# Q's fourth weight block on GpSimd's queue, and ahead of the third in the projection

## The chip, the core and the metric

The kernel runs on one core of a Trainium2 chip. The core has five engines that run side by side and meet through semaphores: TensorE (PE; its weight loads are listed as PEld), VectorE (DVE), ScalarE (ACT), GpSimd (POOL) and SyncE (SP). An engine takes its instructions in the order in which the program gives them, and so does the queue from which an engine issues its transfers. The metric is the device time of one execution in microseconds. All times within an execution count from the start of its span, the time from its first instruction to its last.

## What is computed

Two blocks read the same layer-normalised input, and their sum is added to the input. Block A is linear attention with 32 heads of 16 columns; block B is a gated feed-forward network. All inputs are bf16; S = 2048 rows, D = 512, F = 1792.

```python
xn = _layernorm(x, axis=-1)
return x + _A_ref(xn, A_wqkv, A_wo) + _B_ref(xn, B_w_gate, B_w_up, B_w_down)

# _A_ref: q, k, v = split(x @ wqkv)
phi = lambda t: jnp.where(t > 0, t + 1, jnp.exp(t)) + 1e-6
pq, pk = phi(q), phi(k)
kv = jnp.einsum("bhsd,bhse->bhde", pk, v)
z = jnp.einsum("bhsd->bhd", pk)
num = jnp.einsum("bhqd,bhde->bhqe", pq, kv)
den = jnp.einsum("bhqd,bhd->bhq", pq, z)[..., None] + 1e-6
o = num / den            # then o @ wo

# _B_ref
g = _silu(x @ w_gate)
u = x @ w_up
return (g * u) @ w_down
```

The change lies in q = xn @ wqkv[:, 0:512], for the first two tiles of rows.

## The kernel before

The 2048 rows are worked in 16 tiles of 128. The program is written out by hand: a helper (`K.op`, `K.dma`) appends each instruction to its engine's list in the order of the calls and puts a wait in front of it wherever an operand was written, or a buffer is still read, by another engine. Nothing reorders the lists afterwards; `emit` (L90) writes them out, and each wait is a `wait_ge` on one semaphore. Every DMA has a semaphore of its own.

The first stage loads x and the weights and makes K's and Q's projections. The weight matrix of K, and that of Q, is loaded in blocks of 128 of its 512 rows, since a projection sums over four such blocks: `wqkv_load(eng, h, name, i, c0, n, after)` (L211) loads the n blocks from c0 on, and `xload` (L205) loads tiles of x. Each block of a weight and each lone tile of x is 128 KB. `after` is a list of results that the issue waits for. SP's queue issues, in order: x 0; wk 0 and 1 in one transfer; wk 2; x 2; wq 0; wq 1; x 3; wq 2; wq 3; x 4; x 5; x 6 and 7 in one. ACT's queue issues x 1 and wk 3. GpSimd's queue issues no transfer; its work up to there is four small set-up instructions (L236 to L244), and next on it stand `eps(0)` (L315), `rstd_of(0)` (L325) and `nbias(0)` (L398), which make the scale of tile 0 from the statistics that VectorE takes with `bns` (L299) and `agg` (L302).

The first four tiles take a faster way in than the rest. Their x is centred or corrected but not yet scaled, transposed (into `xcT`), and multiplied with the weights; the scale `rstd` comes in later, when ScalarE reads the product (`first_ek`, `first_pk`, `first_pq`, L579 to L601). `proj_part(t, wname, c, pos)` (L520) is one matmul of 128x512: block c of the weight for tile t. `pos` is its place in the sum over four: 0 clears the PSUM bank, 3 closes it. K's product of tile t lies in bank 2·(t mod 2), Q's in the bank after it. Tile 2 and the ones after it use `proj_first` (L506) and `proj` (L493), which run over the blocks by themselves.

TensorE's order around the change is: K of tile 0 and K of tile 1 (blocks 0, 1, 3, 2), Q's blocks 0 and 1 for tile 1 and then for tile 0, four transposes of tile 2 (`tp_first`, L464), Q's blocks 2 and 3 for both tiles (these four are L731 to L735), then K and Q of tile 2 (L511), and the first accumulation of xn and phi(K) (`gtacc`, L645, matmuls at L649). ScalarE reads Q of tile 0 with `first_pq(0)`, which stands between the last two of the four matmuls in the program.

From tile 4 on a loop projects K and Q of a tile, takes their exponentials, and accumulates. The feed-forward stage (L844 on) and the output (L1038 on) follow. Neither is touched.

Of the kernel before, what the change touches and what calls it, by code (L numbers as in the profile page):

```python
# [109 lines left out]
def bass_parallel_sum__linear_attn_block__swiglu_ffn__prompt_kernel(  # L110
# [13 lines left out]
    pe, act, dve, pool, sp = nc.tensor, nc.scalar, nc.vector, nc.gpsimd, nc.sync  # L124
    bf, f32 = dt.bfloat16, dt.float32

    with contextlib.ExitStack() as es:
# [65 lines left out]
        def bk(i):  # L193
            return ("bank", i)
# [5 lines left out]
        def rows(v, t0, n):  # L200
            if t0 < NLONE:
                return v[t0 * P:(t0 + n) * P, :].rearrange("(t p) d -> p t d", p=P)
            return v[NLONE * P:, :].rearrange("(p t) d -> p t d", t=NT - NLONE)[:, t0 - NLONE:t0 - NLONE + n, :]

        def xload(eng, h, t0, n, after=()):  # L205
            K.dma(
                eng, lambda: h.dma_start(x_sb[:, t0:t0 + n, :], rows(xin, t0, n)),
                r=list(after), w=[("x", t0 + i) for i in range(n)],
            )

        def wqkv_load(eng, h, name, i, c0, n, after=()):  # L211
            K.dma(
                eng,
                lambda: h.dma_start(
                    wqkv_sb[:, c0:c0 + n, i * D:(i + 1) * D],
                    A_wqkv[c0 * P:(c0 + n) * P, i * D:(i + 1) * D].rearrange("(c p) f -> p c f", p=P),
                ),
                r=list(after), w=[(name, c) for c in range(c0, c0 + n)],
            )
# [37 lines left out]
        wqkv_load("sp", sp, "wq", 0, 1, 1)  # L257
        xload("sp", sp, 3, 1)
        wqkv_load("sp", sp, "wq", 0, 2, 1)
        wqkv_load("sp", sp, "wq", 0, 3, 1)  # L260
        xload("sp", sp, 4, 1)
        xload("sp", sp, 5, 1)
        xload("sp", sp, 6, 2)

        cw = nc.const_aps.tensor(1.0, (P, P), bf)
        cx = nc.const_aps.tensor(1.0, (P, 512), bf)
# [35 lines left out]
        def agg(t):  # L302
            K.op("dve", lambda: dve.bn_aggr(mv[:, t, :], stats[:, t, :]), r=[("st", t)], w=[("mv", t)])
# [202 lines left out]
        def proj_first(t, wname, h):  # L506
            lo, b = (D, kb(t)) if wname == "wk" else (0, qb(t))
            K.op(
                "pe",
                [  # L510
                    (lambda c=c: pe.matmul(  # L511
                        banks[b], xcT[:, NDC * t + c, :], wqkv_sb[:, c, lo:lo + D],
                        start=(c == 0), stop=(c == NDC - 1),
                    ))
                    for c in (2 * h, 2 * h + 1)
                ],
                r=[("xcT", t, i) for i in (2 * h, 2 * h + 1)] + [(wname, i) for i in (2 * h, 2 * h + 1)], w=[bk(b)],
            )

        def proj_part(t, wname, c, pos):  # L520
            lo, b = (D, kb(t)) if wname == "wk" else (0, qb(t))
            K.op(
                "pe",
                lambda: pe.matmul(  # L524
                    banks[b], xcT[:, NDC * t + c, :], wqkv_sb[:, c, lo:lo + D],
                    start=(pos == 0), stop=(pos == NDC - 1),
                ),
                r=[("xcT", t, c), (wname, c)], w=[bk(b)],
            )

        def kb(t):
            return 2 * (t % 2)

        def qb(t):
            return 2 * (t % 2) + 1
# [61 lines left out]
        def first_pq(t):  # L597
            K.op(
                "act", lambda: act.activation(pkq[:, t, 1, :], banks[qb(t)], ACT.Identity, scale=rstd[:, t:t + 1]),
                r=[bk(qb(t)), ("rstd", t)], w=[("pq", t)],  # L600
            )  # L601
# [126 lines left out]
        agg(5)  # L728
        bns(6)
        agg(6)  # L730
        proj_part(0, "wq", 2, 2)  # L731
        proj_part(1, "wq", 2, 2)
        proj_part(0, "wq", 3, 3)
        first_pq(0)
        proj_part(1, "wq", 3, 3)  # L735
        proj_first(2, "wk", 0)
        proj_first(2, "wk", 1)
        eps_two(1, "pool")
# [413 lines left out]
```

## Time and profile before

| What | us |
|---|---|
| median of three runs | 210.12 (210.02 to 210.15) |
| the profiled execution's own time | 210.52 |
| its span | 209.3 |
| TensorE busy in it | 205.5 (98%) |
| VectorE / ScalarE / GpSimd busy | 120.1 / 71.0 / 72.1 |

The profile is of one execution. A row of a timeline gives the start, the length, the engine, the line of the program, the operation, what it writes and reads, and how many instructions are merged in the row; in brackets stands how long the engine was idle before it and what ended that. An SPq or ACTq row is the issue of a transfer, and the transfer itself lands later; the list of issues gives the time from the start of the issue to the landing. Matmuls overlap each other in the pipeline, so the length of one (0.38 us for 128x512) is more than the step from one to the next; the ends of matmuls are modelled. Some matmul records can be missing from a trace.

### The profile page before, as it was taken

The numbers are of one execution on the slowest core, as the hardware profiler recorded it, in microseconds if no ns is written. First come the engines' busy times: TensorE is split into PE (matmuls) and PEld (weight loads), VectorE is DVE, ScalarE is ACT, GpSimd is POOL, SyncE is SP. The second block draws the span as 40 slices with busy tenths as digits, with TensorE's granted clock in tenths as the row PEclk, the third lists the DMA queues.
The fourth block names the chain that finished last, engine by engine and source line by source line (L and its number), as shares of the span: only waits on it lengthen the run. The fifth ranks groups of instructions, "written<-read, shape, count | busy, mean of one in ns | idle before, by whom it ended". The sixth has DMA issues, their size and how long they took to land.

```text
span 209.3 us, 2808 instructions
## 1 busy us (share of the span) xinstructions
PE 205.5 (98%) x997; PEld 94.7 (45%) x1016; DVE 120.1 (57%) x246; ACT 71.0 (34%) x125; POOL 72.1 (34%) x91
## 2 busy tenths in 40 slices
PE   8999999999999999999999999999999999999996
PEld 3444444444444444444444444444444444444444
DVE  4899988336365874637355746365556545374122
ACT  4877666966643331312112312213031213121000
POOL 2627977568032543223041422240424132221200
DMA  6764644894796011010201110102011010110101
GB/s 198 228 176 77 128 99 100 253 368 157 204 357 47 12 38 25 28 25 25 52 0 50 28 29 21 50 0 53 6 44 25 27 28 25 49 30 25 50 28 50
DMA packets 30287, 16.84 MB, mean 80 GB/s; under 512 B 20928, under 2 KB 29632, under 8 KB 30272
## 3 DMA queue, kind: packets, MB, share of 16 engines
q1 hardware_dynamic: 29984, 16.39, 30.1%
q10 hardware_dynamic: 288, 0.26, 0.4%
q8 instruction: 8, 0.13, 0.3%
q14 instruction: 7, 0.06, 0.1%
HBM read 9.70 MB, written 2.10 MB: 56 GB/s over the span
## 4 chain that ended last, share of the span: by engine, by line
PE 96%; DVE 2%; issue 1%; POOL 1%; DVEq 0%
PE psum L849 44%; PE psum L1054 23%; PE psum L497 10%; PE psum L1043 7%; PE psum L649 6%; PE psum L524 2%; PE psum L511 2%; PE psum L272 1%; POOL prod L998 1%; PE psum L433 0%; PE psum L421 0%; DVE pkq L573 0%; DVE den L1006 0%; DVE pkq L870 0%; DVE eq L564 0%
## 5 line engine op out<-in xcount | busy, mean ns | idle before, releaser
L864 ACT ACTIVATE sg<-psum 128x512 bf16<-128x512 f32 x56 | 33.4, 598 | 106.0 <-PE psum L849 103.6
L849 PE MATMUL psum<-xnT,wg_sb 128*128 128x512 bf16 x222 | 57.2, 379 | 0.2 <-issue 0.2
L849 PE MATMUL psum<-xnT,wu_sb 128*128 128x512 bf16 x216 | 55.8, 379 | 0.4
L998 POOL TENSOR_TENSOR prod<-pkq,zb 128x512 f32<-128x512 bf16 x16 | 18.6, 1161 | 55.9 <-DVE pkq L573 55.9
L849 PEld LDWEIGHTS psum<-xnT,wu_sb 128*128 128x128 bf16 x224 | 21.9, 98 | 26.4
L849 PEld LDWEIGHTS psum<-xnT,wg_sb 128*128 128x128 bf16 x224 | 21.8, 98 | 26.2 <-issue 0.2
L1067 DVE TENSOR_TENSOR out_sb<-psum,x_sb 128x512 bf16<-128x512 f32 (+2 forms) x17 | 11.2, 660 | 35.9 <-PE psum L1054 35.9
L1022 POOL TENSOR_TENSOR pqn<-pkq,rden 128x512 bf16<-128x512 bf16 x16 | 16.9, 1056 | 36.6 <-DVE rden L1016 36.6
L870 DVE TENSOR_TENSOR pkq<-psum,sg 128x512 bf16<-128x512 f32 x28 | 19.2, 686 | 17.1 <-PE psum L849 14.6
L870 DVE TENSOR_TENSOR xn_sb<-psum,sg 128x512 bf16<-128x512 f32 x28 | 18.8, 671 | 14.2 <-PE psum L849 13.6
L1054 PE MATMUL psum<-wd_sb,xn_sb 128*128 128x512 bf16 (+2 forms) x126 | 25.7, 355 | 0.0
L1054 PE MATMUL psum<-wd_sb,pkq 128*128 128x512 bf16 x108 | 25.1, 379 | 0.2
L497 PE MATMUL psum<-wqkv_sb,xnT 128*128 128x512 bf16 x95 | 22.5, 379 | 0.1
L641 POOL TENSOR_TENSOR zacc<-zacc,pkq 128x512 f32<-128x512 f32 x15 | 17.3, 1156 | 5.0 <-DVE ek L564 4.6
L1054 PEld LDWEIGHTS psum<-wd_sb,xn_sb 128*128 128x128 bf16 x126 | 11.8, 98 | 12.5
L1054 PEld LDWEIGHTS psum<-wd_sb,pkq 128*128 128x128 bf16 x112 | 11.0, 98 | 13.2
L1043 PE MATMUL psum<-m_sb,eq 128*128 128x512 bf16 (+2 forms) x67 | 16.4, 366 | 0.1
L649 PE MATMUL psum<-pkq,xn_sb 128*128 128x512 bf16 x61 | 15.5, 379 | 0.1
L497 PEld LDWEIGHTS psum<-wqkv_sb,xnT 128*128 128x128 bf16 x96 | 9.4, 98 | 11.3
L1006 DVE TENSOR_REDUCE den<-prod 128x32 f32<-128x512 f32 x16 | 10.9, 684 | 5.9 <-POOL prod L998 5.9
L573 DVE SCALAR_TENSOR_TENSOR pkq<-pkq,eq 128x512 bf16<-128x512 bf16 x16 | 11.1, 692 | 0.6
L300 DVE BATCH_NORM_STATS2 stats<-x_sb 128x6 f32<-128x512 bf16 x16 | 10.8, 678 | 0.6 <-DMA x_sb<-in_A_x_dram 0.6
(75 smaller groups left out, 140.0 us busy)
## 6 DMA issues: line engine op xcount, KB each, us to landing
out_dram<-out_sb SPq DMA_DIRECT2D x15, 128.0 KB, 1.7
wg_sb<-in_B_w_gate_dram SPq DMA_DIRECT2D x2, 896.0 KB, 8.1
wu_sb<-in_B_w_up_dram SPq DMA_DIRECT2D x2, 896.0 KB, 6.3
wd_sb<-in_B_w_down_dram SPq DMA_DIRECT2D x1, 1792.0 KB, 11.1
x_sb<-in_A_x_dram SPq DMA_DIRECT2D x5, 256.0 KB, 3.3
x_sb<-in_A_x_dram SPq DMA_DIRECT2D x5, 128.0 KB, 3.2
wqkv_sb<-in_A_wqkv_dram SPq DMA_DIRECT2D x5, 128.0 KB, 3.5
wqkv_sb<-in_A_wqkv_dram SPq DMA_DIRECT2D x1, 512.0 KB, 8.2
```

The source lines that it names most:

```text
L497: (lambda c=c: pe.matmul(banks[b], xnT[:, c, t * P:(t + 1) * P], wqkv_sb[:, c, lo:lo + D], start=(c == 0), stop=(c == NDC - 1),))
L573: lambda: dve.scalar_tensor_tensor(out=dst, in0=src, scalar=0.0, in1=e, op0=ALU.max, op1=ALU.add,),
L641: lambda: pool.tensor_tensor(out=zacc[:, :], in0=zacc[:, :], in1=pk, op=ALU.add),
L649: (lambda c=c: pe.matmul(banks[4 + c], xn_sb[:, t, c * P:(c + 1) * P], pkq[:, t, 0, :], start=(t == 0), stop=(t == NT - 1),))
L849: (lambda c=c: pe.matmul(banks[b], w_sb[:, c, fc * P:(fc + 1) * P], xnT[:, c, C * 512:(C + 1) * 512], start=(c == 0), stop=(c == NDC - 1),))
L864: lambda: act.activation(sg[:, j % NSG, :], banks[gb], ACT.Silu),
L870: lambda: dve.tensor_tensor(out=hT(C, fc), in0=banks[ub], in1=sg[:, j % NSG, :], op=ALU.mult,),
L998: lambda: pool.tensor_tensor(out=p, in0=pkq[:, t, 1, :], in1=zb[:, :], op=ALU.mult),
L1022: lambda: pool.tensor_tensor(out=pqn[:, t % NPN, :].rearrange("p (i g h e) -> p g i h e", i=NB, g=NG, e=DH), in0=pkq[:, t, 1, :].rearrange ...
L1043: (lambda g=g: pe.matmul(dst, pqnT(t)[:, g, :], m_sb[:, g, lo:hi], start=(g == 0), stop=False,))
L1054: (lambda fc=fc: pe.matmul(dst, hT(C, fc)[:, jj * P:(jj + 1) * P], wd_sb[:, fc, lo:hi], start=False, stop=(fc == NFC - 1),))
L1067: lambda: dve.tensor_tensor(out=o, in0=src, in1=x_sb[:, t, lo:hi], op=ALU.add),
```

## The change

The load of Q's fourth block (wq 3) leaves SP's queue, where it stood ahead of x 4, and goes to GpSimd's. There it waits until x 0 has landed. The four matmuls of Q's last two blocks for tiles 0 and 1 change places: block 3 is now the third of the sum, and block 2 the fourth, which closes it.

```diff
         wqkv_load("sp", sp, "wq", 0, 2, 1)
-        wqkv_load("sp", sp, "wq", 0, 3, 1)
         xload("sp", sp, 4, 1)
         xload("sp", sp, 5, 1)
         xload("sp", sp, 6, 2)
+        wqkv_load("pool", pool, "wq", 0, 3, 1, [("x", 0)])
...
-        proj_part(0, "wq", 2, 2)
-        proj_part(1, "wq", 2, 2)
-        proj_part(0, "wq", 3, 3)
+        proj_part(0, "wq", 3, 2)
+        proj_part(1, "wq", 3, 2)
+        proj_part(0, "wq", 2, 3)
         first_pq(0)
-        proj_part(1, "wq", 3, 3)
+        proj_part(1, "wq", 2, 3)
```

The new issue stands behind its four set-up instructions in its list and ahead of `eps(0)`.

## The prediction

> **What bounds the kernel now.** I read the busy times first, then a table of stretches (stretch and its length, then busy us of PE, PEld, DVE, ACT and POOL with instruction counts, granted clock, DMA share, GB/s).
>
> ```profile
> PE 205.5 (98%) x997; PEld 94.7 (45%) x1016; DVE 120.1 (57%) x246; ACT 71.0 (34%) x125; POOL 72.1 (34%) x91
> ```
>
> ```profile
> 4.35:12.00 7.65, 7.60 (x37) 3.55 (x37) 6.75 (x21) 6.28 (x13) 4.62 (x10) 1.00 0.79 228
> 12.00:50.00 38.00, 37.84 (x175) 17.24 (x177) 27.56 (x64) 27.62 (x50) 26.70 (x38) 1.00 0.67 177
> 50.00:100.00 50.00, 49.63 (x271) 22.68 (x275) 30.35 (x55) 15.93 (x28) 15.60 (x15) 1.00 0.34 82
> 100.00:150.00 50.00, 49.74 (x228) 22.64 (x232) 27.58 (x52) 10.16 (x17) 13.04 (x12) 1.00 0.12 30
> 150.00:207.40 57.40, 57.14 (x279) 26.92 (x282) 26.07 (x49) 8.96 (x15) 11.36 (x11) 1.00 0.13 33
> ```
>
> TensorE is busy in all but 1.1 us of the 203 us from 4.35 to 207.40. Busy alone could hide stalls, since matmuls overlap, so I went to the list of waits (engine and line, what it waited for: total, times, longest), asked for PE from 4.5 us to the end. It has one entry:
>
> ```profile
> PE psum L849 <- issue: 0.2, 1, 0.2
> ```
>
> The kernel is therefore bound by TensorE's own rate from its first projection on. An edit that removes no matmul can gain only from a gap ahead of that, or lose by making a new one. Now the place of the edit: the chain of work (start, length, what) and PE's timeline.
>
> ```profile
> 8.24 0.22 PE psum L469 x4
> 8.47 0.86 PE psum L524 x4
> 9.33 1.73 PE psum L511 x8
> ```
>
> ```profile
> 8.25 0.10 PEld L524 LDWEIGHTS psum<-wqkv_sb,xcT 128*128 128x128 bf16 x1
> ...
> 8.57 0.10 PEld L524 LDWEIGHTS psum<-wqkv_sb,xcT 128*128 128x128 bf16 x1 [0.17 <-DMA wqkv_sb<-in_A_wqkv_dram]
> ...
> 8.30 1.03 PE L524 MATMUL psum<-wqkv_sb,xcT 128*128 128x512 bf16 x4
> ```
>
> The four L524 matmuls are wq 2 for tiles 0 and 1, then wq 3 for both: the instructions that the change reorders. They take 0.86 us in the chain, 0.215 each, and the eight after them 1.73, 0.216 each. So the wait for wq 3 that the trace shows (0.17 us at the weight load of 8.57) costs TensorE nothing: that load ends at 8.67, and its matmul is third of the four, due at 8.30 + 2 × 0.216 = 8.73. This is the wait that the change could remove, and it is already hidden, by some 0.06 us.
>
> **The change part by part.** *Removed:* one issue on SP. Its issues stand in these rows (merged where they follow each other; the one of 4.60, wq 3 alone, takes 0.43 us):
>
> ```profile
> 2.23 0.43 SPq L207 DMA_DIRECT2D x_sb<-in_A_x_dram  x1
> 2.70 0.91 SPq L214 DMA_DIRECT2D wqkv_sb<-in_A_wqkv_dram  x2
> 3.65 0.43 SPq L207 DMA_DIRECT2D x_sb<-in_A_x_dram  x1
> 4.12 0.91 SPq L214 DMA_DIRECT2D wqkv_sb<-in_A_wqkv_dram  x2
> ...
> 4.60 0.43 SPq L214 DMA_DIRECT2D wqkv_sb<-in_A_wqkv_dram  x1
> ...
> 5.07 1.39 SPq L207 DMA_DIRECT2D x_sb<-in_A_x_dram  x3
> ```
>
> x 4 to x 7 are issued 5.07 − 4.60 = 0.47 us earlier. VectorE waits for x 4:
>
> ```profile
> 8.90 0.69 DVE L300 BATCH_NORM_STATS2 stats<-x_sb 128x6 f32<-128x512 bf16 x1 [0.59 <-DMA x_sb<-in_A_x_dram]
> ```
>
> Up to 0.47 of that 0.59 may go, but no PE wait hangs on it: worth 0.
>
> *Added on GpSimd:* a wait for x 0 and one issue. x 0 has landed when its first reader starts, 2.95.
>
> ```profile
> 2.95 0.42 DVE L391 SCALAR_TENSOR_TENSOR scr<-x_sb 128x256 bf16<-128x256 bf16 x1 [1.15 <-DMA x_sb<-in_A_x_dram]
> ...
> 1.27 0.29 POOL L244 TENSOR_SCALAR_AFFINE_SELECT ident<-ident 128x128 bf16<-128x128 bf16 x1 [0.20 <-POOL nhalf L240]
> 4.84 0.23 POOL L319 TENSOR_SCALAR vpe<-mv 128x1 f32<-128x1 f32 x1 [3.27 <-DVE mv L303]
> 5.15 0.57 POOL L328 TENSOR_TENSOR rstd<-vpe,nhalf 128x1 f32<-128x1 f32 x1
> ...
> 6.55 0.69 ACT L581 ACTIVATE ek<-psum,rstd 128x512 bf16<-128x512 f32 x1 [0.34 <-PE psum L524]
> ```
>
> Behind it on GpSimd stands eps(0), at 4.84 and waiting 3.27 us for VectorE anyway, then rstd(0), which ends at 5.72. ScalarE's first exp needs it at 6.55 and is released by PE, so it has 0.83 us to spare. The issue is free if GpSimd is through by 4.84 + 0.83 = 5.67, which is 2.7 us after 2.95. The trace shows no issue from this queue. Bounds: 0.43 us (one on SP) and 3.9 us, as if the queue were held until its transfer lands (the longest landing below). I take something near the lower: the issues on both other queues took 0.4 to 0.5, a sixth of the room. Cost 0, with an upper end of 6.85 − 5.67 = 1.2 us.
>
> *Moved: the transfer.* Issues with their time to landing: wk 3 (ACT's, at 1.56), wk 2 (SP's, at 1.72), then x 2, wq 2 and wq 3 (at 2.23, 4.12, 4.60).
>
> ```profile
> wqkv_sb<-in_A_wqkv_dram ACTq DMA_DIRECT2D x1, 128.0 KB, 3.5
> ...
> wqkv_sb<-in_A_wqkv_dram SPq DMA_DIRECT2D x1, 128.0 KB, 3.5
> ...
> x_sb<-in_A_x_dram SPq DMA_DIRECT2D x1, 128.0 KB, 3.2
> ...
> wqkv_sb<-in_A_wqkv_dram SPq DMA_DIRECT2D x1, 128.0 KB, 3.6
> ...
> wqkv_sb<-in_A_wqkv_dram SPq DMA_DIRECT2D x1, 128.0 KB, 3.9
> ```
>
> At 3.2 to 3.9 us the new wq 3 would land at 6.2 to 6.9; its first weight load is now the one of 8.25. Reserve at least 1.4 us. The Trainium skill (DMA: Bandwidth & Descriptors, section Anatomy of one DMA — SWDGE (gpsimd) path) puts a transfer from GpSimd at about 2.0 us plus bytes over 436 GB/s; by that it would land near 5.3, an estimate, and the sum would be the same zero. No row here shows such a transfer.
>
> *Moved past others.* wq 3's 128 KB now share the DMA engines with what SP queued before it. How full these are:
>
> ```profile
> 3.00:4.00 1.00, 1.00 (x10) 0.81 (x10) 0.89 (x5) 0.23 (x2) 0.00 (x0) 1.00 0.99 326
> 4.00:5.00 1.00, 1.00 (x8) 0.55 (x6) 0.96 (x3) 0.49 (x3) 0.16 (x1) 1.00 1.14 347
> 5.00:6.00 1.00, 1.00 (x4) 0.40 (x3) 0.96 (x3) 0.56 (x2) 0.81 (x3) 1.00 0.96 311
> ```
>
> At 347 GB/s 128 KB take 0.38 us, so each transfer still under way is late by 0 to 0.38. Its users:
>
> ```profile
> 5.37 0.36 PEld L524 LDWEIGHTS psum<-wqkv_sb,xcT 128*128 128x128 bf16 x2 [0.28 <-issue]
> ...
> 5.59 0.15 PEld L524 LDWEIGHTS psum<-wqkv_sb,xcT 128*128 128x128 bf16 x1
> ...
> 6.83 0.68 DVE L300 BATCH_NORM_STATS2 stats<-x_sb 128x6 f32<-128x512 bf16 x1
> ```
>
> wk 3 lands at 5.06 and is loaded at 5.37; wk 2 at 5.22, loaded at 5.59: with the full 0.38 both come at most 0.1 us late. x 2 (landing 5.43, read 0.03 later) and x 3 (read at 6.83) may delay VectorE, by 0.38 at most, but it idles 0.59 at 8.90. wq 2 lands at 7.72, at most 8.10, and is now second in order, needed at 8.57. Cost 0 to 0.1 us; I take 0.05, since wk 3 has been under way for over a microsecond before wq 3 can start.
>
> *The swap on TensorE* is the same four matmuls into the same banks: 0. **Sum:** 0 + 0 + 0 + 0.05 on the profiled execution's 210.52 us (span 209.3 and 1.2 around it). The median of the three runs is 0.4 us lower, and the difference is carried to it: 210.12 + 0.05, about 210.2.
>
> **The rivals.** *GpSimd is held (slower).* Place: eps(0) behind the issue. Point: when the issue keeps the engine over 2.7 us. Then rstd(0), ScalarE's exp and everything serial behind it move, and PE waits at L511 for ScalarE's copies. With the upper end 3.9 us the price is 1.2, so 211.3. For it: no issue of this queue in the trace, and nothing else on GpSimd between 1.56 and 4.84 that would tell. Against it: all issues shown are a sixth as long as the room. A stronger form: the first issue loads code. Held twice the longest landing, 7.8 us, it would cost 7.8 − 2.7 = 5.1, or 215.2. The Trainium skill (GPSIMD Engine Reference, section 2.1 Instruction dispatch) gives about 6 us for the first call of a freshly loaded kernel; by that the price is an estimate of 3.3 us. The trace does not bear it out where it could: the affine select at 1.27 began 0.20 us after its input. I give it little.
>
> *wq 3 lands late (slower).* It is now first in order. From 5.3 us after 2.95 on, each further us is lost on TensorE; at 6.0 us (the longest landing, 3.9, plus the shortest here, 2.1, as if it queued behind a whole other transfer) it is 0.7, so 210.8. The shortest, x 0:
>
> ```profile
> x_sb<-in_A_x_dram SPq DMA_DIRECT2D x1, 128.0 KB, 2.1
> ```
>
> *The DMA engines lose more than the bytes (slower).* If the mix of two streams costs SP's train 0.8 us instead of 0.38, wk 3 is 0.5 us late at 5.37: 210.6. For it: share 0.96 to 1.14, no room left.
>
> *Faster.* The unprofiled runs are 0.4 us shorter than the profiled one, so their loads may stand otherwise, and wq 3 may hold TensorE there. The most that can come back is the issue slot, 0.47: 209.65. Against it: a zero wait in the profile.
>
> **How the numbers follow.** Forecast 0.45 (its own range 209.9 to 210.5); GpSimd held 0.22, of which 0.04 for code loading; DMA engines losing more 0.12; wq 3 late 0.08; faster 0.13. The bound of 0.2% is 0.42 us, about what a measurement of this kernel tells from no change. A little of the DMA case stays under it and a little of the forecast's cases lie over it, which cancel; some 0.02 of the faster case stays under it: faster 0.11, same 0.47, slower 0.42. The range leaves out some 0.07 below (most of the gain of a whole slot) and 0.1 above (GpSimd held past 4.2 us): 209.7 to 211.6.
>
> **What would show it.** Right: PE's waits from 4.5 us on still a single entry, the four L524 matmuls again at 0.86 us, eps(0) near 4.84, the transfer from GpSimd landing by 7 and the x 4 statistics starting before 8.90. Wrong: eps(0) after 5.7 (GpSimd held); the weight load of 8.25 released by a DMA (wq 3 late); the loads of 5.37 or 5.59 later by over 0.1 (contention); a first projection before 4.35, which nothing here foresees.

## The result, and the profile after

The changed kernel takes 210.63 us, the median of 21 runs (209.93 to 211.09), against 210.26 us for 21 runs of the kernel before (209.83 to 210.72). The ratio is 1.0017, with a 95% interval of 1.0009 to 1.0025: 0.37 us slower. That stays under the 0.42 us that the prediction counted as no change, yet the interval leaves 1.0 out, so there is a small loss to explain. A second series of the same kernel, told below, gave 1.0017 again.

The profiled execution took 211.09 us, with a span of 209.9. The same stretch as before, from the page's view of stretches (stretch and length, then busy us of PE, PEld, DVE, ACT and POOL with counts, granted clock, DMA share, GB/s):

```profile
4.35:12.00 7.65, 7.04 (x35) 3.29 (x34) 6.93 (x21) 5.68 (x12) 4.67 (x10) 1.00 0.69 203
```

TensorE lost 0.56 us of busy time in these 7.65 us (7.60 to 7.04). The list of its waits from 4.5 us to the end has one entry, and PE's timeline places it:

```profile
PE psum L524 <- DMA wqkv_sb<-in_A_wqkv_dram: 0.6, 1, 0.6
```

```profile
5.09 0.59 PE L524 MATMUL psum<-wqkv_sb,xcT 128*128 128x512 bf16 x1 [0.61 <-DMA wqkv_sb<-in_A_wqkv_dram]
...
6.33 2.50 PE L524 MATMUL psum<-wqkv_sb,xcT 128*128 128x512 bf16 x10
8.67 0.39 PE L469 MATMUL psum<-ident,xc_sb 128*128 128x128 bf16 x4
8.89 1.03 PE L524 MATMUL psum<-wqkv_sb,xcT 128*128 128x512 bf16 x4
9.75 1.89 PE L511 MATMUL psum<-wqkv_sb,xcT 128*128 128x512 bf16 x8
```

In this execution the first projection starts at 5.09 instead of 4.35. It waited for wk 0 and 1, which SP issues at 1.26, as before; their landing went from 3.0 to 3.7 us after the issue. The chain of waits (start, length, what) runs through that transfer:

```profile
1.26 3.70 DMA wqkv_sb<-in_A_wqkv_dram
4.96 0.14 issue
5.09 0.59 PE psum L524
...
9.05 0.86 PE psum L524 x4
9.92 1.73 PE psum L511 x8
```

Its last two pieces are those that the prediction read: the reordered four matmuls wait for nothing and again take 0.86 us, the eight after them 1.73. Two of the rows below are new: GpSimd's issue on its timeline, and its transfer in the list of issues (KB, us to landing).

```profile
3.23 0.78 POOL L214 DMA_DIRECT2D wqkv_sb<-in_A_wqkv_dram  x1 [1.66 <-DMA x_sb<-in_A_x_dram]
4.86 0.23 POOL L319 TENSOR_SCALAR vpe<-mv 128x1 f32<-128x1 f32 x1 [0.85 <-DVE mv L303]
```

```profile
wqkv_sb<-in_A_wqkv_dram SPq DMA_DIRECT2D x1, 256.0 KB, 3.7
...
wqkv_sb<-in_A_wqkv_dram POOLq DMA_DIRECT2D x1, 128.0 KB, 3.9
```

GpSimd is through with the issue at 4.01, 1.66 us before the point at which the prediction let it matter, and `eps(0)` starts at 4.86 (before: 4.84). wq 3 lands at 3.23 + 3.9, about 7.1. VectorE's statistics of x 2, x 3 and x 4:

```profile
5.73 0.69 DVE L300 BATCH_NORM_STATS2 stats<-x_sb 128x6 f32<-128x512 bf16 x1 [0.18 <-DMA x_sb<-in_A_x_dram]
...
7.42 0.69 DVE L300 BATCH_NORM_STATS2 stats<-x_sb 128x6 f32<-128x512 bf16 x1 [0.24 <-DMA x_sb<-in_A_x_dram]
...
8.83 0.69 DVE L300 BATCH_NORM_STATS2 stats<-x_sb 128x6 f32<-128x512 bf16 x1
```

x 4 comes earlier (8.83, before 8.90) and x 3 later (7.42, before 6.83).

### The profile page after: what moved, and what is told of

It reads as the page before. It is cut to its first block, busy times and chain, and to the rows that moved or that the text cites. A ratio compares the mean times of both kernels' runs of the same rounds, so it can differ in the third digit from the quotient of the medians.

```text
span 209.9 us, 2827 instructions
## 1 busy us (share of the span) xinstructions
PE 206.5 (98%) x1016; PEld 94.6 (45%) x1016; DVE 120.9 (58%) x246; ACT 71.0 (34%) x125; POOL 72.8 (35%) x92
## 4 chain that ended last, share of the span: by engine, by line
PE 97%; DMA 2%; SPq 0%; DVE 0%; issue 0%
PE psum L849 46%; PE psum L1054 23%; PE psum L497 10%; PE psum L1043 7%; PE psum L649 7%; PE psum L524 2%; DMA wqkv_sb<-in_A_wqkv_dram 2%; PE psum L511 2%; PE psum L956 0%; PE psum L433 0%; SPq L207 0%; PE psum L979 0%; DVE out_sb L1067 0%; PE psum L469 0%
## 5 line engine op out<-in xcount | busy, mean ns | idle before, releaser
L849 PE MATMUL psum<-xnT,wu_sb 128*128 128x512 bf16 x224 | 57.5, 379 | 0.0
```

The costliest lines, as they stand in the source:

```text
L849: (lambda c=c: pe.matmul(banks[b], w_sb[:, c, fc * P:(fc + 1) * P], xnT[:, c, C * 512:(C + 1) * 512], start=(c == 0), stop=(c == NDC - 1),))
```

## One time per execution: when TensorE reaches tile 2's transposes

One reading helps with every profile below. Call T0 the start of the four transposes of tile 2 (L469). These are its row in the profile before, the row ahead of it, and the row of K of tile 3, which is used below:

```profile
5.58 2.66 PE L524 MATMUL psum<-wqkv_sb,xcT 128*128 128x512 bf16 x10
8.08 0.39 PE L469 MATMUL psum<-ident,xc_sb 128*128 128x128 bf16 x4
...
11.76 1.89 PE L511 MATMUL psum<-wqkv_sb,xcT 128*128 128x512 bf16 x8
```

T0 was 8.08 before and is 8.67 after. The executions' own times are 210.52 and 211.09, so from T0 to the end they take 202.44 and 202.42: the same, although T0 moved by 0.59. The table gives T0 and the own time of the profiled executions with the usual warm-up. What the last column has above 202.42 was lost behind T0, to within some 0.02.

| Kernel (below) | first projection | T0 | own time | own time − T0 |
|---|---|---|---|---|
| before | 4.35 | 8.08 | 210.52 | 202.44 |
| after | 5.09 | 8.67 | 211.09 | 202.42 |
| again (changed, 2nd series) | 4.36 | 7.62 | 210.24 | 202.62 |
| sp_swap | 4.37 | 8.44 | 210.85 | 202.41 |
| act_x0 | 4.37 | 8.23 | 210.70 | 202.47 |
| dup | 4.42 | 8.44 | 210.84 | 202.40 |
| x3_late | 4.36 | 7.80 | 210.50 | 202.70 |
| x3_first | 4.63 | 7.74 | 210.30 | 202.56 |
| split | 4.27 | 8.09 | 210.50 | 202.41 |
| pool_wk | 4.52 | 7.32 | 210.94 | 203.62 |

T0 varies by more than the first projection does. The reason is in the step between matmuls. In before the ten L524 matmuls from 5.58 to T0 take 2.50 us, in after 2.34 (6.33 to 8.67), in again 2.16 (5.46 to 7.62, row below). At 0.216 a step, ten take 2.16. So again ran them all at that rate; before and after ran one or two at about twice the step, 0.43. TensorE begins an execution at the 0.43 step and goes over to 0.216 at a moment that differs from one execution to the next: in these profiles it is as early as 4.5 us (pool_wk) and as late as 6.9 (sp_swap, dup). In before it is 6.35, in after 6.7, in again 5.35. The granted clock in the view of stretches says 1.00 all the while. The change is not needed for this: before_warm and after_warm, told below, run the same matmuls without a pause from 0.83 us on and ahead of every load, and yet go over at 3.74 and 5.84.

The Trainium skill (TensorE: Matmul & The Clock Gate, Part 1: The HAM clock gate) describes this: half the clock until a free-running window of some 3.4 us has seen TensorE busy, so that the number of slow matmuls varies from run to run. These traces agree with the steps (0.43, then 0.216) and with the variation. The length fits less well: in before_warm the step changes 2.9 us after TensorE's first matmul (0.83 to 3.74).

So the profile on which the prediction rests was one execution with a rather late moment. By the table, a run of the kernel before at 209.83 would have T0 at 209.83 − 202.42 = 7.41 if it loses nothing later; that is an inference, since no such run was profiled. Every operand behind the first projection would be wanted there up to 0.7 us sooner than in the profile of before.

## The experiments

The expectations name their theories by letters and say there what each means. The main ones are these. G: GpSimd's issue itself disturbs the queues' first transfers, as the late wk 0 and 1 suggested. O: the order of blocks 2 and 3 costs the time. B, later made sharper as E: 128 KB put ahead of SP's queue make the loads behind them later, whoever issues them, and by E that costs TensorE only in executions whose 0.216 step begins early, since only these want the loads so soon. X (x 3 late, and with it the transposed x 3 that K of tile 3 multiplies) and W (wq 0 and wq 1 late) are two places of E. S: single DMA engines that bring their share of a transfer late (told at the end), made more likely by the change.

**again.** The changed kernel as it is, profiled and timed a second time.

> The changed kernel a second time. In its first profile wk 0 and 1 landed at 4.96 us instead of 4.22, and the first projection began at 5.10 instead of 4.35. Theory G (making the descriptors on GpSimd, 3.2 to 4.0 us, holds up one DMA engine's share of wk 0 and 1): landing again near 5.0, first projection near 5.1, ratio to before 1.001 to 1.0025. Theory C (that landing scatters between executions whatever the kernel, and the first profile hit a late one): landing anywhere from 4.1 to 5.0, ratio between 0.999 and 1.0015.

Measured: 210.53 (210.24 to 211.04, 12 runs), ratio 1.0017 (1.0006 to 1.0027). PE's timeline, and below it PEld's:

```profile
5.46 2.32 PE L524 MATMUL psum<-wqkv_sb,xcT 128*128 128x512 bf16 x10
7.62 0.39 PE L469 MATMUL psum<-ident,xc_sb 128*128 128x128 bf16 x4
```

```profile
6.95 0.34 PEld L524 LDWEIGHTS psum<-wqkv_sb,xcT 128*128 128x128 bf16 x3 [0.31 <-DMA wqkv_sb<-in_A_wqkv_dram]
...
11.48 0.56 PEld L511 LDWEIGHTS psum<-wqkv_sb,xcT 128*128 128x128 bf16 x4 [0.51 <-ACT kpos L587]
```

The first projection is back at 4.36 with GpSimd's issue in its place (3.24, 0.78 us), so the issue does not always hold wk 0 and 1 back, and yet the series is as slow as the first. G lost its main witness. Theory C (the landing scatters whatever the kernel) has the landing right, but by it the change itself costs nothing, and two series at 1.0017, both with intervals above 1, speak against that. This execution has an early 0.216 step, and it shows a loss that after's profile does not have. The weight load of wq 1 waits 0.31 us and comes just in time: its matmul starts at 6.97, where the step puts it. The wait of 11.48 costs 0.20 (202.62 against 202.42). The row names kpos, which ScalarE had finished at 11.11; what came last is tile 3's transposed x 3, a transfer of its own, which lands at 11.37. It is 3.8 us behind x 3's statistics, here as in before (6.83 to 10.63):

```profile
7.57 0.69 DVE L300 BATCH_NORM_STATS2 stats<-x_sb 128x6 f32<-128x512 bf16 x1 [0.69 <-DMA x_sb<-in_A_x_dram]
```

In before and after K of tile 3 begins 3.68 us behind T0. With T0 at 7.62 that would be 11.30, and the transposed tile lands at 11.37. In before's profile it landed 1.1 us ahead (10.63 against 8.08 + 3.68 = 11.76). In after's it was 1.1 as well (11.23 against 12.35), because T0 itself was late there.

**sp_swap.** The order alone: wq 3 ahead of wq 2 on SP, the matmuls changed places, nothing on GpSimd.

```diff
-        wqkv_load("sp", sp, "wq", 0, 2, 1)
         wqkv_load("sp", sp, "wq", 0, 3, 1)
+        wqkv_load("sp", sp, "wq", 0, 2, 1)
...
-        proj_part(0, "wq", 2, 2)
-        proj_part(1, "wq", 2, 2)
-        proj_part(0, "wq", 3, 3)
+        proj_part(0, "wq", 3, 2)
+        proj_part(1, "wq", 3, 2)
+        proj_part(0, "wq", 2, 3)
         first_pq(0)
-        proj_part(1, "wq", 3, 3)
+        proj_part(1, "wq", 2, 3)
```

> Block 3 of Q is loaded on SP ahead of block 2, and the four matmuls are swapped as in the change; GpSimd issues nothing. Theory G: landing of wk 0 and 1 near 4.2, ratio 1.000 within 0.001. Theory O (the order of the matmuls, or what follows from it, costs the time): ratio 1.0017. Theory C: landing scatters from 4.1 to 5.0, ratio within 0.0015 of 1.

Measured: 210.22 (209.89 to 210.93, 12 runs), ratio 1.0006 (0.9994 to 1.0018). PE's timeline:

```profile
5.81 2.79 PE L524 MATMUL psum<-wqkv_sb,xcT 128*128 128x512 bf16 x10
8.44 0.39 PE L469 MATMUL psum<-ident,xc_sb 128*128 128x128 bf16 x4
8.66 1.03 PE L524 MATMUL psum<-wqkv_sb,xcT 128*128 128x512 bf16 x4
```

The ten matmuls take 2.63 us to T0, since the step changes only at 6.9, and behind T0 nothing is lost (202.41). The reordered four follow without a wait. Runs down to 209.89 occur, as with the kernel before. The interval alone can't part it from 1.0017, but 8 of its 12 runs lie below 210.42, the fastest run of act_x0 below, and nothing in the trace speaks for a cost of the order.

**act_x0.** As the change, but wq 3 is issued from ACT's queue.

```diff
-        wqkv_load("sp", sp, "wq", 0, 3, 1)
...
+        wqkv_load("act", act, "wq", 0, 3, 1, [("x", 0)])
```

(and the matmuls as in sp_swap)

> Block 3 is issued from ACT's queue when x 0 has landed, the matmuls swapped: the same early transfer without GpSimd. Theory G: wk 0 and 1 land near 4.2, ratio 1.000 within 0.001. Theory B (a further 128 KB issued at 3 us takes its share of the DMA engines, from whichever queue): landing later than 4.6, ratio 1.0015 or more.

Measured: 210.70 (210.42 to 211.09, 11 runs), ratio 1.0022 (1.0011 to 1.0033). It is as slow as the change, with no transfer from GpSimd. PE's timeline, and below it PEld's, which waits for wq 0 and wq 1; they land at 7.22 and 7.52 (before: 5.95 and 6.33):

```profile
5.65 2.74 PE L524 MATMUL psum<-wqkv_sb,xcT 128*128 128x512 bf16 x10
8.23 0.39 PE L469 MATMUL psum<-ident,xc_sb 128*128 128x128 bf16 x4
```

```profile
7.26 0.10 PEld L524 LDWEIGHTS psum<-wqkv_sb,xcT 128*128 128x128 bf16 x1 [0.63 <-DMA wqkv_sb<-in_A_wqkv_dram]
7.56 0.33 PEld L524 LDWEIGHTS psum<-wqkv_sb,xcT 128*128 128x128 bf16 x3 [0.21 <-DMA wqkv_sb<-in_A_wqkv_dram]
```

Its 0.216 step began at 5.65, and still T0 is 8.23: the ten matmuls from 5.65 took 2.58 instead of 2.16. Not all of that is the added bytes. In x 2, wq 0 and wq 1 of this execution one of the 16 DMA engines is 0.7 to 1.0 us behind the other 15, which had wq 0 in at 6.18 and wq 1 at 6.84. The ratio is what B expected; the late landing of wk 0 and 1 that B expected with it did not come (4.14).

**dup.** The kernel before, with one more 128 KB load of the same block from GpSimd into a buffer that nothing reads. Its computation is that of before; the last wait of SP takes in the added load.

```diff
+        gscr = sb("gscr", [D])
+        K.dma("pool", lambda: pool.dma_start(gscr[:, :], A_wqkv[3 * P:4 * P, 0:D]), r=[("x", 0)], w=[("gscr",)])
```

> The kernel before, with SP's loads and the matmuls as they were, and one more load of the same 128 KB block into an unused buffer from GpSimd when x 0 has landed. Theory G: wk 0 and 1 land near 5.0, ratio 1.001 to 1.003. Theory B: everything of SP's queue behind 5 us is 0.4 us later as well, ratio 1.002 to 1.004, with a wait of TensorE for wq 3. Theory C and theory O: ratio within 0.0015 of 1.

Measured: 210.64 (210.23 to 210.84, 11 runs), ratio 1.0015 (1.0005 to 1.0025). The order of the blocks and SP's list are those of before, so the cost comes with the additional early transfer. wk 0 and 1 land at 4.29, not at 5.0 as G expected, and the wait for wq 3 that B expected is not there: the profile itself, with its late step (6.9), loses nothing behind T0. So this trace does not show where the cost falls.

These four divide the change: the order costs nothing that shows, the engine that issues makes no difference that shows, and each version with the early 128 KB is slower by 0.15 to 0.22%. How the runs are spread:

| Kernel | runs | below 210.2 us | above 210.7 us |
|---|---|---|---|
| before, all series | 112 | 55 | 8 |
| sp_swap | 12 | 5 | 2 |
| changed, both series | 33 | 2 | 11 |
| act_x0 | 11 | 0 | 5 |
| dup | 11 | 0 | 4 |
| x3_late | 12 | 1 | 3 |

Half of the runs of before lie below 210.2, and 6% of the changed kernel's. Theory E says that the short executions should lose, and they did become rare; but there are more above 210.7 too. If every run of before were 0.37 us longer, 1 of the 112 would lie below 210.2 and 39 above 210.7, nearly the shares of the changed kernel. So the table shows a loss and does not tell E from a cost that every execution pays.

**x3_late.** The kernel before, with x 3 and wq 2 exchanged on SP, so that x 3 alone is late.

```diff
-        xload("sp", sp, 3, 1)
         wqkv_load("sp", sp, "wq", 0, 2, 1)
+        xload("sp", sp, 3, 1)
```

> The kernel before with x 3 and wq 2 exchanged in SP's queue: x 3 lands near 7.7 us, everything else as before or earlier, no transfer added. Theory X (x 3 late, so the transpose of tile 3 lands after 11.2 us and TensorE waits at tile 3 of K in executions where its rate doubles early): ratio 1.001 to 1.0025, no run below 210.2. Theory W (wq 0 and wq 1 late): ratio 1.000 within 0.0008. Theory S (single late DMA engines in the first weights): ratio 1.000.

Measured: 210.54 (210.17 to 210.91, 12 runs), ratio 1.0007 (0.9996 to 1.0018). The ratio is inconclusive: it lies below the 1.001 that X expected, its interval reaches up to 1.0018, and one run is below 210.2. The trace shows the place, without a wait for a weight block; DVE's row, then PEld's:

```profile
7.81 0.69 DVE L300 BATCH_NORM_STATS2 stats<-x_sb 128x6 f32<-128x512 bf16 x1 [0.86 <-DMA x_sb<-in_A_x_dram]
```

```profile
10.67 0.55 PEld L649 LDWEIGHTS psum<-pkq,xn_sb 128*128 128x128 bf16 x4 [0.38 <-POOL pkq L606]
11.74 0.34 PEld L511 LDWEIGHTS psum<-wqkv_sb,xcT 128*128 128x128 bf16 x3 [0.52 <-ACT kpos L587]
```

The transposed x 3 lands at 11.63. T0 + 3.68 is 11.48 here, the load starts at 11.74, and the execution loses 0.28 behind T0 (202.70). Of these, 0.07 are lost earlier, at 10.67: the first accumulation waits for GpSimd's product of tile 0, which waits for VectorE (L564), which stands behind x 3's statistics. A late x 3 does cost TensorE, in two ways. The fastest run is 210.17, where before reaches 209.83 in the same series.

**x3_first.** The opposite: x 3 ahead of wq 0 and wq 1.

```diff
+        xload("sp", sp, 3, 1)
         wqkv_load("sp", sp, "wq", 0, 0, 1)
         wqkv_load("sp", sp, "wq", 0, 1, 1)
-        xload("sp", sp, 3, 1)
```

> The kernel before with x 3 ahead of wq 0 and wq 1 in SP's queue: wq 0 lands near 6.4 and wq 1 near 6.8, x 3 near 6.0, no transfer added. Theory W (wq 0 and wq 1 late, and TensorE waits for them where its rate doubles early): ratio 1.001 to 1.002. Theory X: ratio 1.000 or a little below. Theory S: 1.000.

Measured: 210.30 (210.19 to 210.36, 11 runs), ratio 1.0000 (0.9991 to 1.0008). Now the two blocks are late instead (PEld):

```profile
6.64 0.10 PEld L524 LDWEIGHTS psum<-wqkv_sb,xcT 128*128 128x128 bf16 x1 [0.30 <-DMA wqkv_sb<-in_A_wqkv_dram]
7.07 0.33 PEld L524 LDWEIGHTS psum<-wqkv_sb,xcT 128*128 128x128 bf16 x3 [0.34 <-DMA wqkv_sb<-in_A_wqkv_dram]
```

The 0.216 step began at 4.6 with the first projection (4.63). In pool_wk, fast from its first projection too, T0 comes 2.80 later (4.52 to 7.32), which would be 7.43 here, and it is 7.74; 0.2 of the difference is the wait for wq 1 at 7.07. Another 0.14 is lost behind T0 (202.56), at 14.15, where TensorE waits for a product of VectorE, which had idled 0.51 us for x 4. The time neither falls nor rises, as X and S expected; W expected 1.001 to 1.002. Why its runs lie within 0.17 us, when those of before are spread over 1.1, stays open.

**split.** The kernel before, with wk 0 and wk 1 in a transfer each. This makes later issues of SP 0.47 us later without a byte more.

```diff
-        wqkv_load("sp", sp, "wk", 1, 0, 2)
+        wqkv_load("sp", sp, "wk", 1, 0, 1)
+        wqkv_load("sp", sp, "wk", 1, 1, 1)
```

> The kernel before with wk 0 and wk 1 in two transfers on SP instead of one; all later issues of SP move 0.47 us back. If the landing of wk 0 and 1 sets the first projection (4.35 us, 0.09 after TensorE is free), it begins at 4.27 to 4.30 and the ratio is 0.9993 to 1.000; if the later loads were already just in time (theories X and W together), their 0.47 us shows and the ratio is 1.0005 to 1.002.

Measured: 210.60 (210.44 to 211.12, 12 runs), ratio 1.0016 (1.0008 to 1.0025). Moving the later loads back costs about what the change costs. In the profile the first projection starts at 4.27, but its second block is 0.4 us late, and wq 0 and wq 1 are waited for at 7.11 and 7.42 (0.29 and 0.22). It mixes two causes, and so doesn't prove E.

**pool_wk.** wq 3 from GpSimd when wk 0 and 1 have landed, with the order of the matmuls as before. It was to free the first loads of the new transfer.

```diff
-        wqkv_load("sp", sp, "wq", 0, 3, 1)
...
+        wqkv_load("pool", pool, "wq", 0, 3, 1, [("wk", 0)])
```

> GpSimd issues block 3 of Q only when wk 0 and 1 have landed (about 4.2 us instead of 3), and the matmuls keep the order of before, block 3 last. Its bytes then move from about 6.2 us on, behind x 2, wq 0, wq 1 and most of x 3. Theory E (the early 128 KB delays what SP's queue loads between 5 and 7.5 us): these land as in the kernel before (wq 1 by 6.8, x 3 by 7.2), ratio 1.000 within 0.0008. Theory A (another queue's transfer costs 0.3 us wherever it stands): ratio 1.0015.

Measured: 211.07 (210.32 to 212.56, 11 runs), ratio 1.0034 (1.0016 to 1.0051). Neither expected ratio fits. wq 1 (6.53) and x 3 (7.03) land as early as E expected, but wq 2 lands at 8.07, with one DMA engine 0.7 us behind the rest, and wq 3 at 9.13, and the weight loads wait for both (PEld):

```profile
8.11 0.11 PEld L524 LDWEIGHTS psum<-wqkv_sb,xcT 128*128 128x128 bf16 x2 [0.58 <-DMA wqkv_sb<-in_A_wqkv_dram]
...
9.17 0.11 PEld L524 LDWEIGHTS psum<-wqkv_sb,xcT 128*128 128x128 bf16 x2 [0.95 <-DMA wqkv_sb<-in_A_wqkv_dram]
```

That is 1.2 us behind T0 (203.62), 0.57 of it for wq 2 and 0.62 for wq 3. It tells nothing between the theories, but it prices the rival of a late wq 3: with an issue 1.45 us later (4.68 instead of 3.23) it comes about.

**before_nofill and after_nofill.** Both kernels without the five warm-up matmuls (`fill(5, 512)`), which feed no output. If TensorE's fast step always began late, E leaves the change no cost.

```diff
-        fill(5, 512)
```

> The kernel before without its five warm-up matmuls. TensorE should then keep its slow step (0.43 us a matmul) well past 8 us, so that all loads are early for it. Together with after_nofill: theory E (the change only takes away time that TensorE needs where its rate doubles early) says the two medians agree within 0.1 us; theory S (single late DMA engines in the first weights, wk 0 to 3, made more likely by the change) says that the changed one stays 0.3 to 0.4 us above.

> The changed kernel without the five warm-up matmuls: theory E, the median of before_nofill within 0.1 us; theory S, 0.3 to 0.4 us above it.

Measured: 211.29 (210.23 to 213.35) and 211.30 (210.31 to 212.07), 12 runs each. The slow step was expected to last well past 8 us. In the profiles the rate doubles at 7.3 and 6.9 instead, hardly later than in sp_swap and dup, and neither loses anything behind T0 (8.60 and 8.40; own times 211.01 and 210.82). The change then costs 0.01 us between the medians, which is what E says. But the ratios, 1.0052 (1.0027 to 1.0076) and 1.0045 (1.0028 to 1.0063), are uncertain by more than the 0.0017 in question, so the pair can't tell E from a loss of 0.37 us.

**before_warm and after_warm.** Both kernels with 24 warm-up matmuls ahead of the first load, and nine instead of five later, so that the fast step is there from the first projection on.

```diff
+                (lambda: pe.matmul(banks[3][:, :], cw, cx[:, :], start=True, stop=True))
+                for _ in range(24)
...
-        xload("sp", sp, 0, 1)
+        xload("sp", sp, 0, 1, [("warmed",)])
...
-        fill(5, 512)
+        fill(9, 512)
```

> The kernel before with 24 warm-up matmuls ahead of the first load, and nine more while it is under way, so that the first projection always runs at the fast step (0.216 us). About 8 us longer than before; scatter between executions smaller than the 0.9 us of before, since the moment of the doubling no longer matters. Beside after_warm it shows what the change costs where TensorE is fast from the start.

> The changed kernel with the same long warm-up. Theory E: 0.4 to 0.8 us above before_warm, more than the 0.35 us of the plain pair, with waits of TensorE for wq 1 and for the transpose of tile 3. Theory S: 0.3 to 0.4 us, as in the plain pair, and all of it at the first K projections.

Measured: 218.61 (217.91 to 218.92, 4 runs) and 218.72 (217.75 to 220.26, 6 runs). Holding the loads back until TensorE is warm costs 8 us. The scatter did not shrink as expected, since the 24 matmuls end and release the loads the later, the later the step changes (at 3.74 and 5.84; first issues at 7.65 and 8.66). The pair's difference of 0.11, where E expected 0.4 to 0.8, drowns in it. The traces say a little more. From the first projection to T0 the two take 2.81 and 2.80 us, so neither waits for wq 0 or wq 1, against E's expectation. Behind T0 the changed one loses 0.15 us waiting for wq 3 and 0.06 at K of tile 3. The other loses nothing there, but 0.72 later, for tile 4's transposed x. One execution of each does not say how often.

## Why the prediction came out as it did

*The bound.* TensorE's rate from its first projection on: confirmed, with the addition that the rate itself changes at a moment that varies. "A first projection before 4.35" did not come in the changed kernel; one at 5.09 did. With it came the sign "the loads of 5.37 or 5.59 later by over 0.1": the first of them stands at 6.12 in after. It had moved with wk 0 and 1, and not by contention at wk 3; in again it stands at 5.35.

*Removed.* SP's slot: x 4's statistics at 8.83, worth nothing to TensorE, as said. *GpSimd's issue* at nothing: right. It takes 0.78 us where 0.43 was taken, and `eps(0)` starts 0.02 later. Both forms of the rival that holds GpSimd fall: the engine is held for neither 3.9 nor 7.8 us. *The moved transfer:* 3.9 and 4.0 us to landing, the upper end of 3.2 to 3.9 and a little over; the landings at 7.12 and 7.26 lie past the foretold 6.2 to 6.9 and 1.8 us and more past the other estimate, 5.3. They are still ahead of the 8.89 and 7.84 at which the block is used, in again by 0.58 instead of "at least 1.4". *The swap* at nothing: right, as far as sp_swap can tell.

*Moved past others, taken at 0.05 and measured at 0.37.* This is the step that failed. It priced the transfers that the 128 KB pass. That they do it is shown by act_x0 and dup; how the 0.37 comes about is shown in part. Three things in the step were wrong.

First, the size: "each transfer still under way is late by 0 to 0.38", 128 KB at 347 GB/s. Landings in us, read from each transfer's last semaphore update:

```
        wk 0,1  wk 3   wk 2   x 2    wq 0   wq 1   x 3    wq 2
before   4.22   5.04   5.22   5.42   5.95   6.33   6.66   7.76
after    4.96   5.16   5.36   5.70   6.05   6.55   7.39   7.72
again    4.22   5.00   5.20   5.41   6.19   6.91   7.54   7.89
```

The view of stretches shows more bytes moved from 6 to 7 us, before, after and then again (same columns as above):

```profile
6.00:7.00 1.00, 1.00 (x5) 0.45 (x4) 0.93 (x5) 0.66 (x2) 0.56 (x3) 1.00 0.91 204
```

```profile
5.00:6.00 1.00, 0.91 (x3) 0.43 (x4) 0.79 (x3) 0.07 (x1) 0.81 (x3) 1.00 1.07 348
6.00:7.00 1.00, 1.00 (x5) 0.45 (x4) 0.93 (x4) 0.70 (x2) 0.39 (x2) 1.00 0.93 284
```

```profile
6.00:7.00 1.00, 1.00 (x7) 0.35 (x5) 0.80 (x4) 0.95 (x3) 0.60 (x3) 1.00 1.00 345
```

Before, 311 GB/s moved from 5 to 6 us. wq 1 and x 3 are late by up to 0.58 and 0.88. The new transfer's packets move from 5.2 to 6.8 us in the trace of after and from 5.3 to 6.9 in again, so it is these it meets, and not wk 3 and wk 2, which stayed within 0.14. Part of the delay is that of one DMA engine. Fifteen of the 16 had brought x 3 by 6.64 before, 7.29 after and 7.10 in again, and wq 1 by 6.32, 6.41 and 6.85. So in again 0.46 of x 3's 0.88 is common to them, not far from the 0.38 of the prediction, and the rest is the last engine's. An estimate: with x 3 at 7.10, the transposed tile would be there near 10.93 (0.03 to the statistics, 3.80 more), ahead of the 11.30 at which it was due. So the 0.20 that again lost needed both.

Second, the users. wq 0 and wq 1 were not priced at all. x 3's delay was set against VectorE's idle time at 8.90, but x 3 has two other ways to TensorE: through its transpose into K of tile 3, and through VectorE and GpSimd to tile 0's product (0.07 in x3_late). Idle time on VectorE behind it gives nothing back there.

Third: the cover was read from one execution in which TensorE's fast step began at 6.35. With that moment, 1.1 us lay ahead of tile 3, and dup's own profile, with a late step, loses nothing behind T0. In the profiles with an earlier moment the cover is gone: 0.20 lost in again, 0.28 in x3_late, about 0.4 in act_x0 ahead of T0, there with the late engine in it. That the early moments make the short half of the runs, and that the loss sits there, is inferred.

The rival "the DMA engines lose more than the bytes" had the right kind of mechanism and, at 210.6, the right time, in the wrong place (wk 3): that the time agrees is luck. "wq 3 lands late" occurred in neither profile of the changed kernel, but in after_warm (0.15). "Faster" did not come. The range held the time because it was wide; the forecast's own range, to 210.5, did not.

*What stays open.* How the 0.37 divides between wq 0 and wq 1, tile 3, and late first weights as in after's profile, where 0.74 was lost at 5.09 to a single late DMA engine. Theory S was not put to a test of its own: no run shows whether the early transfer makes late engines more frequent, and the losses in after, act_x0 and again all have one in them. Nor is it shown that only executions with an early moment pay. No profile of the kernel before happened to have an early moment, so its short executions were inferred from their times and the 202.42. And none of the versions tried beats the kernel before; x3_first equals it.

## What to carry to other kernels

Slack read from one profile is the slack of that execution: where the bounding engine reaches a point at different times from run to run, price a delay by the earliest of them, which the shortest runs show. A transfer moved forward can be paid for by those it passes, here by wq 1 and x 3; follow each of these to every reader, transposes included. Where a program's times scatter, compare how many runs fall below a mark as well as the medians: here that showed the loss more plainly than any single trace, though not its cause.

## What the runs showed of the hardware

The step of TensorE, 0.43 us and then 0.216 for a 128x512 matmul, goes over at 4.5 to 6.9 us in the profiles with the usual warm-up matmuls, with a granted clock of 1.00 shown throughout. In the table T0 lies between 7.3 and 8.7, and the rest takes 202.4 to 202.7 us in all but pool_wk. A spread of that size in T0 would be enough for the 1.1 us over which the runs of before are spread.

Each of these transfers ends with 16 semaphore updates, one for each of the 16 DMA engines, and in most profiles the last of the 16 comes well behind the other 15: in the transfer of wk 0 and 1 of after at 4.96, when the 15th was in at 4.09. Others:

```
sp_swap        wk 3   15th at 5.07, 16th at 5.68
act_x0         x 2            5.73         6.61
after_nofill   x 2            5.41         6.22
x3_late        wq 2           6.58         7.44
before         wq 2           7.34         7.76
```

It comes with a transfer from GpSimd and without one (sp_swap, x3_late and before have none), at a different transfer each time. GpSimd's packets in after start at 5.2 us, behind the 4.96, so they can't have filled that engine. What makes it late is not shown by these traces.

A 128 KB transfer from GpSimd's queue took 3.9 and 4.0 us from issue to landing, 0.78 of it on the engine, with its first packets 1.2 and 1.3 us after that. The Trainium skill (DMA: Bandwidth & Descriptors, section Issuing engines are not separate DMA queues) says that transfers run on the same 16 engines whichever engine starts them, and that starting them on several saves only the time to issue; act_x0 and dup agree (1.0022 and 1.0015 beside 1.0017).
